# Adding x outside TensorE for 15 of 16 block groups, with six output copies on VectorE and a re-made order of steps

## The chip, the cores and the metric

The kernel runs on one core of one Trainium2 chip. The metric is the device time of one execution in microseconds (us). Every comparison below was made on one chip, with the kernel before and the other kernel in the same rounds. For one core no second core shows whether a run was disturbed, so a run counts as slow if it is over 1.5% above the fastest of its kernel, and only the other runs are compared.

## The reference

An attention without a softmax over pairs, followed by a gated layer:

```python
q_s = exp(q - max_d q);  q_s = q_s / (sum_d q_s + 1e-09)      # q, k, v: 8 x 8 x 576 x 64
k_s = exp(k - max_s k);  k_s = k_s / (sum_s k_s + 1e-09)
kv  = einsum('bhsd,bhse->bhde', k_s, v)
x   = einsum('bhsd,bhde->bhse', q_s, kv)                       # then 4608 rows x 512
H = maximum(x @ w_h, 0);  T = 1 / (1 + exp(-(x @ w_t + b_t)))
out = T * H + (1 - T) * x
```

## The kernel before

The kernel keeps x turned, with its 512 columns on partitions in four blocks, and handles the 8 batches in four pairs. Rows that don't fill a tile are done at the end as chunks 8 and 9. The gate is computed as out = x + (tanh + 1) * dd. The `blend` step writes the second term to `g`. The output tile is then turned back by matmuls with the identity, and the term x comes in at one of two places: either an elementwise addition (`add_x`) puts it into `g` first, or TensorE accumulates it with a second matmul for each block (`xs` in `turn_block`). `added(g)` lists the blocks of pair `g` that take the first way.

```python
added = lambda g: ((0, 1), (0, 1, 2), (0, 1, 2), (0, 1, 2, 3))[g]

def add_x(c, ob):
    xv, gv = views(c)
    eng = nc.vector if (c, ob) == (B - 1, 3) else nc.gpsimd
    eng.tensor_add(gv(ob), gv(ob), xv(ob))

def turn_block(t, k_, xs, us):
    dst = t[:, k_, :]
    if xs is not None:
        mm(dst, xs, ident, True, False)          # x, by TensorE
    mm(dst, us, ident, xs is None, True)

def out_tile(g, n, spare=False):
    ...
    for k_ in range(4):
        turn_block(t, k_, None if k_ in added(g) else xT[g][:, k_, n]..., gT[g][:, k_, n]...)
```

Other parts are these:

```python
def q_scale_p(b, n0, n1):                        # scaling of exp(q), on GpSimd
    e, r = eq[b][:, n0:n1], qsum[b][:, n0:n1]
    nc.gpsimd.tensor_mul(e, e, r.broadcast_to(list(e.shape)))

def q_turn(b, n0, n1):                           # batches 6 and 7: turned by DMA
    nc.sync.dma_start_transpose(out=qsD[b]..., in_=eq[b][:, n0:n1]...)

def load_bias():
    nc.sync.dma_start(brow, moe_b_t.rearrange("(k p) -> k p", p=P))   # 2 KB

def gate_bias():                                 # one small matmul on TensorE
    nc.tensor.matmul(t, brow, id4, is_transpose=True, ...)
    nc.vector.tensor_scalar_mul(bt2, t, 0.5)

def warm_up(n):                                  # fillers: results are not used
    for _ in range(n):
        mm(warm, ident, wide, True, True)
```

A list `order` of some 560 steps fixes the order of instructions by hand. Each engine works through its own steps in that order.

The softmax here doesn't subtract the row's maximum and nothing guards it: scores larger than these inputs give would overflow.

## Time and profile before

| | before |
|---|---|
| median of 3 runs | 125.06 us (124.79 to 125.07) |
| profiled run | 124.45 us, span 122.5 us, mean granted TensorE clock 0.999 |
| busy share: TensorE, VectorE, ScalarE, GpSimd | 91%, 78%, 76%, 65% |
| matmuls, VectorE, ScalarE, GpSimd instructions | 1371, 179, 130, 75 |
| sums of batch 1 (k by v) start | 28.11 us |
| first product from transposed q of batch 6 | 85.04 us |
| first 512-column product of batch 7 | 95.18 us |
| last matmul of the output starts | 118.13 us |

In the profile, PE is TensorE's matmul, PEld its weight load, DVE is VectorE, ACT ScalarE, POOL GpSimd, SP the engine that issues most transfers. `qsD` is transposed q of batches 6 and 7, `px` their product with kv, `psk` the sums over k and v, `pt` and `ph` the two halves of the gate, and `nat` an output tile. In a timeline a row is a group of like instructions, and the bracket at its end is the idle time of that engine before it and what ended it. For the last rows of the table I read TensorE's timeline.

### The profile page before, as it was taken

To read this page: it belongs to the slowest core of one execution; us is meant where nothing else is said; L and a number is where in the kernel's file an instruction comes from. 1 tells how busy PE (TensorE), PEld (TensorE's weight loads), DVE (VectorE), ACT (ScalarE), POOL (GpSimd) and SP (SyncE) were. 2 spreads that over 40 slices of the span, in tenths; PEclk is the share of its full clock that TensorE was granted. 3 is DMA by queue.
4 is the path that set the end of the run, shared out by engine and by line. 5 is a ranking of instruction groups with operands and counts; after the bars stand their busy time and mean duration, and the time that the engine had idled before them with its cause. 6 is when DMAs were issued, how large, how long until landed. Compare 5 with 4: busy or idle time off the path is not lost.

```text
span 122.5 us, 3361 instructions
## 1 busy us (share of the span) xinstructions
PE 111.3 (91%) x1371; PEld 61.5 (50%) x1371; DVE 95.9 (78%) x179; ACT 92.9 (76%) x130; POOL 79.8 (65%) x75
## 2 busy tenths in 40 slices
PE   4998985998999998999997999997999999999960
PEld 1344543354336444745745464454456545599830
DVE  1079796579999999999979996898656379779960
ACT  4193737496979998789979999983986895588650
POOL 2000487952279989599899899996995307934620
PEclk9999999999999999999999999999999999999999
DMA  3999999999999999999999999999977500539995
GB/s 100 388 402 408 409 399 397 410 412 411 406 412 409 402 411 412 415 398 416 417 356 404 411 411 401 418 212 246 438 171 214 219 0 0 206 144 390 423 384 175
DMA packets 20583, 41.24 MB, mean 337 GB/s; under 512 B 5460, under 2 KB 5976, under 8 KB 19544
## 3 DMA queue, kind: packets, MB, share of 16 engines
q1 hardware_dynamic: 20568, 41.03, 89.0%
q8 instruction: 10, 0.16, 0.5%
q14 instruction: 5, 0.04, 0.1%
HBM read 30.41 MB, written 9.44 MB: 325 GB/s over the span
## 4 chain that ended last, share of the span: by engine, by line
DMA 51%; PE 28%; ACT 5%; POOL 5%; SPq 3%; DVE 3%; issue 2%; ACTq 0%; POOLq 0%
DMA q<-in_q_dram 24%; DMA k<-in_k_dram 12%; PE ph L64 11%; DMA w32h<-in_moe_w_h_dram 9%; PE pt L64 9%; DMA qsD<-eq 6%; PE nat L64 5%; ACT eq L174 4%; SPq L94 3%; POOL eq L254 3%; POOL g L424 2%; PE px L64 1%; DVE r L224 1%; ACT xT L357 1%; PE psk L64 1%
## 5 line engine op out<-in xcount | busy, mean ns | idle before, releaser
L64 PE MATMUL pt<-xT,w16t 128*128 128x512 f16 x128 | 32.9, 380 | 0.4 <-ACT xT L361 0.3
L254 POOL TENSOR_TENSOR eq<-eq,r 128x1024 f16<-128x1024 f16 (+2 forms) x16 | 29.9, 1876 | 4.7 <-DVE r L242 1.6
L64 PE MATMUL ph<-xT,w16h 128*128 128x512 f16 x128 | 32.5, 379 | 0.4 <-DVE dd L405 0.2
L424 POOL TENSOR_TENSOR g<-g,xT 128x512 f16<-128x512 f16 x23 | 26.0, 1154 | 7.1 <-DVE g L413 4.9
L392 ACT ACTIVATE pt<-pt,bt 128x512 f32<-128x512 f32 (+1 forms) x40 | 24.8, 632 | 6.2 <-PE pt L64 5.2
L413 DVE SCALAR_TENSOR_TENSOR g<-pt,dd 128x512 f16<-128x512 f32 (+1 forms) x40 | 24.9, 632 | 4.9 <-ACT pt L392 4.3
L405 DVE SCALAR_TENSOR_TENSOR dd<-xT,ph 128x512 f16<-128x512 f16 x32 | 21.1, 677 | 6.7 <-PE ph L64 6.6
L174 ACT ACTIVATE eq<-q 128x1152 f16<-128x1152 f32 x16 | 18.3, 1168 | 7.1 <-DMA q<-in_q_dram 7.1
L185 POOL CAST v<-v 128x1152 f16<-128x1152 f32 x12 | 13.7, 1154 | 13.2 <-DMA v<-in_v_dram 12.8
L64 PEld LDWEIGHTS <-w16h 128*128 128x128 f16 x160 | 14.5, 98 | 13.2 <-issue 1.6
L64 PEld LDWEIGHTS <-w16t 128*128 128x128 f16 x160 | 14.3, 98 | 12.7 <-issue 1.1
L224 DVE TENSOR_REDUCE r<-eq 128x18 f32<-128x1152 f16 x12 | 16.0, 1345 | 6.0 <-ACT eq L174 6.0
L464 ACT COPY o<-nat 128x512 f32<-128x512 f32 x28 | 16.8, 601 | 4.4 <-PE nat L64 3.5
L174 ACT ACTIVATE ek<-k 128x1152 f16<-128x1152 f32 x16 | 18.4, 1175 | 1.6 <-DMA k<-in_k_dram 1.5
L64 PE MATMUL warm<-wide,ident 128*128 128x512 f16 x53 | 15.1, 427 | 1.8 <-DVE wide L144 1.8
L64 PE MATMUL nat<-ident,g 128*128 128x128 f16 x142 | 14.9, 219 | 0.2 <-DVE o L485 0.2
L64 PEld LDWEIGHTS <-g 128*128 128x128 f16 x144 | 11.4, 98 | 4.8 <-issue 0.5
L357 ACT CAST xT<-px 128x1024 f16<-128x1024 f32 x10 | 10.3, 1034 | 1.8 <-PE px L64 1.8
L64 PEld LDWEIGHTS <-ident 128*128 128x128 f16 x58 | 5.6, 106 | 8.4 <-issue 3.4
L69 PE MATMUL pq<-ident,eq 128*128 128x128 f16 x108 | 9.0, 219 | 0.9 <-DVE x L309 0.4
L274 DVE COPY qsT<-pq 128x1024 f16<-128x1024 f16 (+1 forms) x18 | 9.7, 542 | 0.0
L69 PEld LDWEIGHTS <-eq 128*128 128x128 f16 x108 | 7.1, 97 | 5.0 <-POOL eq L254 1.1
(53 smaller groups left out, 102.9 us busy)
## 6 DMA issues: line engine op xcount, KB each, us to landing
out_dram<-o SPq DMA_DIRECT2D x8, 1024.0 KB, 5.5
q<-in_q_dram SPq DMA_DIRECT2D x7, 1152.0 KB, 13.9
k<-in_k_dram SPq DMA_DIRECT2D x7, 1152.0 KB, 12.9
v<-in_v_dram SPq DMA_DIRECT2D x5, 1152.0 KB, 14.6
v<-in_v_dram SPq DMA_DIRECT2D x6, 576.0 KB, 11.7
q<-in_q_dram SPq DMA_DIRECT2D x2, 576.0 KB, 4.0
k<-in_k_dram SPq DMA_DIRECT2D x2, 576.0 KB, 6.7
w32h<-in_moe_w_h_dram SPq DMA_DIRECT2D x4, 256.0 KB, 9.9
```

The source lines that it names most:

```text
L64: mm = lambda o, l, r, st, sp: nc.tensor.matmul(o, l, r, start=st, stop=sp, skip_group_check=True)
L69: nc.tensor.matmul(o, i, ident, is_transpose=True, start=True, stop=True, skip_group_check=True,)
L174: nc.scalar.activation(dst[b][:, :, 2 * a : 2 * a + 2, :], in32[which][b][:, 2 * a : 2 * a + 2].rearrange("p c n d -> p n c d"), AF.Exp,)
L185: nc.gpsimd.tensor_copy(o, i)
L224: nc.vector.reduce_sum(qsum[b][:, :, h], eq[b][:, :, h, :], axis=AX.X)
L254: nc.gpsimd.tensor_mul(e, e, r.broadcast_to(list(e.shape)))
L357: copy[how](dst, t.rearrange("p c (n d) -> p c n d", d=64))
L392: nc.scalar.activation(ps, ps, AF.Tanh, bias=bt2[:, ob : ob + 1], scale=0.5)
L405: nc.vector.scalar_tensor_tensor(dd, xv(ob), -0.5, ps, op0=ALU.mult, op1=ALU.max)
L413: nc.vector.scalar_tensor_tensor(gv(ob), th, 1.0, dd, op0=ALU.add, op1=ALU.mult)
L424: eng.tensor_add(gv(ob), gv(ob), xv(ob))
L464: copy(rows_of_four((g, n // 4))[:, n % 4, :], nat.pop((g, n)))
```

## The change

The intent is to take work off TensorE, the busiest engine. x is added by an elementwise engine for all blocks but block 3 of the last pair. Four of these additions go to VectorE and the others to GpSimd. Six of the large output copies (of 32; four before) are done by VectorE, and the list of steps is made anew near the old places.

```diff
+    copy_by = {"A": nc.scalar.copy, "V": nc.vector.tensor_copy}
 ...
-    added = lambda g: ((0, 1), (0, 1, 2), (0, 1, 2), (0, 1, 2, 3))[g]
+    added = lambda g: (
+        (0, 1, 2, 3),
+        (0, 1, 2, 3),
+        (0, 1, 2, 3),
+        (0, 1, 2),
+    )[g]
-    def add_x(c, ob):
+    def add_x(c, ob, eng="P"):
         xv, gv = views(c)
-        eng = nc.vector if (c, ob) == (B - 1, 3) else nc.gpsimd
-        eng.tensor_add(gv(ob), gv(ob), xv(ob))
+        by[eng].tensor_add(gv(ob), gv(ob), xv(ob))
 ...                                    (order: all of it is re-made; the places that matter)
-        ("exp_half", 0, "q", 1), ("load_bias",), ("warm_up", 24), ("load", 1, "q"),
-        ("load", 0, "v", 2), ...
+        ("load", 1, "q"), ("load", 0, "v", 2), ("exp_half", 0, "k", 0), ...
+        ("q_trans", 0, 0), ("cast_v", 0, 0), ("load_bias",), ("q_copy", 0, 0),
+        ("gate_bias",), ("load_weight", "h", "k32", 4), ("load_weight", "t", "q32"),
 ...
+        ("kv_norm", 6), ("q_sums", 7, 0), ("carry", 5, 3), ("add_x", 4, 0, "P"), ...
+        ("q_recip", 7), ("q_scale_p", 7, 4, 9), ("out_tile", 1, 2), ("out_copy", 1, 2, "V"),
+        ("q_turn", 7, 4, 9), ("x_pair", 6, 0, True), ("diff", 5, 2), ("add_x", 4, 3, "P"),
+        ("q_scale_p", 7, 0, 4), ("exp_half", 7, "k", 0), ...
```

## The prediction

> **What bounds the kernel now.** I read, in this order: the page's busy shares and slices, the chain of waits that ended last, the groups of instructions, and the timelines of TensorE and GpSimd.
>
> ```profile
> PE 111.3 (91%) x1371; PEld 61.5 (50%) x1371; DVE 95.9 (78%) x179; ACT 92.9 (76%) x130; POOL 79.8 (65%) x75
> ...
> PE   4998985998999998999997999997999999999960
> ...
> POOL 2000487952279989599899899996995307934620
> ...
> DMA  3999999999999999999999999999977500539995
> ```
>
> TensorE is full nearly everywhere, GpSimd is full from about 35 to 90 us, and DMA is full only until about 80 us. So three limits lie close together, and the stage matters. The chain of waits gives the stages:
>
> ```profile
> 32.33 14.60 DMA k<-in_k_dram
> 46.93 15.05 DMA q<-in_q_dram
> ...
> 77.49 7.51 DMA qsD<-eq
> ...
> 85.04 0.22 PE px_l L64 x2
> ...
> 116.61 0.46 ACT pt L392
> ...
> 118.11 0.48 ACT o L485
> ```
>
> Loads rule up to 62 us; GpSimd's scaling of batch 6 and its DMA transposes stand before 85.0; from there to 116.6 the chain is TensorE alone, without a wait. The 31.6 us from 85.0 to 116.6 can shrink only by less TensorE work, or by starting earlier.
>
> Was TensorE already saturated before 85 us? Its timeline, where the last bracket is real idleness:
>
> ```profile
> 21.80 2.47 PE L64 MATMUL pt<-xT,w16t 128*128 128x512 f16 x8
> 65.25 0.41 PE L64 MATMUL px<-qsT,kvn 64*64 64x512 f16 x4 [0.89 <-ACT xT L357]
> 85.04 0.22 PE L64 MATMUL px_l<-qsD,kvn 64*64 64x64 f16 x2 [0.70 <-DMA qsD<-eq]
> 111.97 1.06 PE L64 MATMUL nat<-ident,g 128*128 128x128 f16 x16
> 112.87 1.47 PE L64 MATMUL ph<-x,w16h 128*128 128x256 f16 x12
> ```
>
> The starts matter, not the modelled ends. Sixteen output matmuls start at 111.97 and the next group at 112.87: 0.90/16 = 56 ns each. I added start-to-start gaps beyond the streaming time of every group (216 ns for a 512-column matmul, as 0.86 us per four in the chain): from the first gate at 21.8 us to the last output matmul at 118.1 us they come to roughly 6 to 7 us (about half of it gaps of 0.1 us after short groups). So TensorE has been the backlog since about 22 us; work taken off it counts, if its inputs come no later.
>
> **What the Trainium skill says.** (1) "TensorE: Matmul & The Clock Gate", Back-to-back issue gap: a warm matmul of N columns takes N/2.4 GHz plus about 2.5 ns, 56 ns at N=128; the page also gives about 81 ns in a stream with weight loads. The trace agrees with 56 ns. (2) "SBUF — State Buffer": VectorE and GpSimd share a port pair under an exclusive lock, and a VectorE instruction with two SBUF inputs contends with a GpSimd instruction that reads SBUF. The trace fits: the sum tree's second add took 0.42 us at 16.73 us but 1.13 us at 14.06 us, beside a GpSimd cast. So a VectorE add of x may cost 0.42 us or over 1 us. (3) "DMA: Bandwidth & Descriptors", HWDGE ordering: each engine's ring is consumed in order. Loads land in their order of issue here too, so an earlier issue of an output delays what is behind it.
>
> **The change part by part.**
>
> ```profile
> L424 POOL TENSOR_TENSOR g<-g,xT 128x512 f16<-128x512 f16 x23 | 26.0, 1154 | 7.1 <-DVE g L413 4.9 <-PE px L64 2.3
> L424 DVE TENSOR_TENSOR g<-g,xT 128x512 f16<-128x512 f16 x1 | 0.4, 418 | 0.0
> L464 DVE COPY o<-nat 128x512 f32<-128x512 f32 x4 | 2.6, 682 | 0.0
> L64 PE MATMUL nat<-ident,xT 128*128 128x128 f16 x32 | 6.2, 219 | 0.0
> ```
>
> *TensorE.* x is added by TensorE today for blocks 2 and 3 of the first pair and block 3 of the next two: 4 blocks x 8 tiles = the 32 matmuls of the last row. After, only block 3 of the last pair is left: 8. That removes 24 x 56 ns = **1.34 us**. (The row's 219 ns is latency, and 6.2 us would be wrong.) Of these, 16 go before about 78 us, 16 more from pairs two and three, and 8 are added in the end stage. Fillers after the first real work go from 3 pairs to 1 (4 x 216 ns = 0.9 us) and 2 at the end go; fillers partly fill waits, so I count **0.4 us**.
>
> *GpSimd.* Pair adds rise from 24 to 30, of which VectorE gets 4 instead of 1: GpSimd 23 to 26, 3 x 1.154 = +3.5 us, and one head cast more (+0.75 us). Up to the scaling of batch 6 it has 12 adds instead of 10, so about +3.0 us with the cast. Its idle stretch before 32.79 us (4.5 us) takes two adds, 2.3 us; the rest must come out of about 2.8 us of small waits between 44 and 77 us. I expect that scaling to end at 76 to 79 us (now 77.0), so the transposes land near 84.5 us (now 85.0): a gain of **0.2 us**, with a real risk of a loss.
>
> *VectorE and ScalarE.* VectorE: 3 adds x 0.418 = 1.25 us more; big output copies 4 to 6 and one fewer of the small row's, about +0.7 us; two weight casts leave (-1.2 us), x copies and remainder copies about cancel. ScalarE: two weight casts come (+1.2 us), two output copies go (-1.2 us), one 1.03 us copy of x goes. After 85 us ScalarE is busy 3.4 to 4.4 of every 5 us until 115 us and VectorE 2.6 to 4.9, so I count this as off the path there.
>
> *The new order at the start.* This is my main doubt. Now:
>
> ```profile
> 21.35 1.62 POOL L117 CAST w16t<-w32t 128x512 f16<-128x512 f32 x2 [0.86 <-DMA w32t<-in_moe_w_t_dram]
> 22.93 1.90 POOL L254 TENSOR_TENSOR eq<-eq,r 128x1024 f16<-128x1024 f16 x1
> ```
>
> Before these, at 18.20 us, GpSimd had already scaled the first part of batch 1. After, both weight casts stand ahead of both scalings. The weights still land near 21.3 us (same bytes ahead of them), so casts end at 22.97, the first scaling at 24.9, the second, with a head cast between, at 27.4 us. ScalarE has its two casts of the same weights ahead of the last copy of x, so the first gate can start only at 23.6 us, not 21.8; then TensorE meets a transpose that waits until 24.9. Walking on by hand, the sums of batch 1's k and v start at about 30.3 instead of 28.1 us with the same six gate and carry groups done. So **+2.0 us** early. It is not all lost: now there are waits later for data and for full engines (0.89 and 0.70 us above, some 1.5 us of smaller ones after 28 us), and a TensorE that is late finds its inputs ready. I let **1.7 us** be absorbed.
>
> *Loads.* The last v load stands after the batch 6 transposes now (issued at 81.65 us or later); after, all loads are ahead of all outputs, landing by about 78 us: 31.45 MB moved by 80 us in the stretches now, against 29.7 MB of loads and weights. It helps batches 5 and 7, but TensorE didn't wait for those. Counted as zero.
>
> Sum: -1.34 - 0.4 - 0.2 + 2.0 - 1.7 = -1.64 us; 125.06 - 1.6 = **123.4 us**.
>
> **The rivals.** *GpSimd becomes the bound.* For it: nearly full from 35 to 90 us, 1.15 us per add against 56 ns x 8 = 0.45 us of TensorE for what each two adds replace per block. Against: it idles from 96 to 102 us and at 28 to 33 us. If each of its extra adds delays the transposes, they land 2 to 3 us later and the result is 125 to 126 us. *The late start is not absorbed:* then all 2.0 us stand, and it is 125 us. *Everything fits better:* if TensorE reaches batch 6's product with its inputs ready at 82 us, only the shorter rest (33.1 us from 85.04 to the last output matmul at 118.1, less 0.5 us net of the removed and added matmuls there) follows, and it is 121 to 122 us. A drain of outputs at the end is unlikely to matter: DMA stands idle around 98 to 105 us, and the same four large outputs follow.
>
> **Range and chances.** The terms that I sized by hand (2.0, 1.7, 0.2) can each be off by 1 us or so, about 1.5 us together. 8 in 10: 121.6 to 125.4 us. Two per cent faster is under 122.56 us, half a spread below my value: 0.28. Slower by 2% (127.56 us) needs two rivals at once: 0.04. Within: 0.68.
>
> **What would show it.** The x matmuls of the output tiles should number 8. The first gate should start near 23.6 us, after a wait for ScalarE's copy of x, and a transpose wait for GpSimd to 24.9 us. Batch 6's second scaling should end at 76 to 79 us; the first product from transposed q should start near 84.5 us. From there to the last matmul it should be 32 to 33 us without waits. The prediction fails if GpSimd waits stand in the chain after 85 us (slower), or if the first gate starts no later than now (faster).

## The result, and the profile after

The changed kernel took 124.31 us as the median of 4 runs (124.20 to 124.61), against 125.06 us (124.79 to 125.14) for the kernel before. The ratio is 0.9947, with a 95% interval of 0.9925 to 0.9970. Every ratio in this document is the mean time of one kernel's fast runs over that of the other's of the same rounds, so it is not quite the ratio of the medians quoted beside it. The time lies in the predicted range, but the gain is 0.66 us by the ratio (0.75 us by the medians), and not the 1.64 us of the sum.

The page of the changed kernel shows the following busy times, slices and costliest group:

```profile
PE 109.6 (89%) x1335; PEld 60.3 (49%) x1335; DVE 97.1 (79%) x177; ACT 93.0 (76%) x134; POOL 83.8 (68%) x79
...
PE   4999067999899999899999999999999899999920
...
POOL 2000096887549999999999999958999128736600
PEclk9999955589999999999999999999999999999997
...
L429 POOL TENSOR_TENSOR g<-g,xT 128x512 f16<-128x512 f16 x26 | 29.9, 1166 | 8.3 <-DVE g L414 6.8
```

TensorE lost 36 matmuls, 24 for x and 12 fillers. GpSimd gained 4 us of work, with 26 additions in the place of 23 and each as long as before. What the prediction did not expect is in the PE and PEclk rows. In slices 5 to 8 (12 to 25 us) TensorE stands still, and then works at half its clock. The groups by line have these two rows:

```profile
L64 PE MATMUL nat<-ident,xT 128*128 128x128 f16 x8 | 1.8, 219 | 0.0
...
L429 DVE TENSOR_TENSOR g<-g,xT 128x512 f16<-128x512 f16 x4 | 3.1, 777 | 0.0
```

Eight matmuls for x are left, as intended. The four additions on VectorE take 777 ns on average, and not the 418 ns of the one that stood in the kernel before.

Here is the start in TensorE's timeline:

```profile
15.59 0.26 PE L135 MATMUL bias_t<-id,brow 4*128 4x4 f32 x1 [3.04 <-DMA brow<-in_moe_b_t_dram]
...
19.28 1.20 PE L64 MATMUL psk<-v,ek 64*64 64x65 f16 x72 [1.61 <-DVE qsT L274]
...
22.85 2.00 PE L64 MATMUL pt<-xT,w16t 128*128 128x512 f16 x4
...
30.75 0.44 PE L64 MATMUL psk<-v,ek 64*64 64x65 f16 x30
```

The first gate starts at 22.85 us, later than before (21.80) but sooner than predicted (23.6). The sums of batch 1 start at 30.75 us, 2.64 us later than before. However, the reason is another than the predicted weight casts. TensorE waits 3.04 us for the 2 KB of the bias. The new order issues that load behind q of batch 1 and v of batch 0. The four starts at 22.85 us take 1.8 us to the next group where they would take 0.86 us at full clock. The stretches of TensorE's granted clock give 0.51 for 15 to 20 us and 0.50 for 20 to 25 us, and 1.00 in both before.

The Trainium skill ("TensorE: Matmul & The Clock Gate", Part 1: The HAM clock gate) says that an idle window of about 3.4 us takes TensorE's clock to half, and about 3.4 us of sustained work brings it back. The trace fits this roughly. In finer stretches half clock begins at 15.1 us, 2.6 us into the wait of 3.04 us, so less idleness than 3.4 us was enough here. It ends at 25.4 us. The return took longer, about 10.2 us, with the second wait of 1.61 us in between.

The chain of waits that ended last shows where the rest went. These are pieces of it:

```profile
4.50 11.04 DMA brow<-in_moe_b_t_dram
...
82.91 0.42 DVE kvn L213
83.33 1.26 DVE r L224
84.59 0.59 DVE dd L406
85.19 0.30 DVE r L242
...
85.62 2.33 POOL eq L254
87.95 1.29 POOL g L429
89.24 1.86 POOL eq L254
...
91.13 4.30 DMA qsD<-eq
...
95.47 0.41 PE px L64 x4
```

Before, this chain held the transposes of batch 6 (they ended at 85.0 us) and TensorE alone after that. Now it holds those of batch 7. VectorE's sums of batch 7's q release GpSimd's first scaling at 85.62 us. GpSimd then does an addition of x (1.29 us), then the second scaling, then the DMA transposes take 4.30 us. TensorE's first full product of batch 7 waits for them. The addition in the middle is block 3 of batch 4, one of those that the change took off TensorE.

An addition at this place is not new in itself. The kernel before had one there too, of block 0 of batch 5, as its GpSimd timeline shows:

```profile
83.74 1.91 POOL L254 TENSOR_TENSOR eq<-eq,r 128x1024 f16<-128x1024 f16 x1 [1.22 <-DVE rz L212]
85.60 1.15 POOL L424 TENSOR_TENSOR g<-g,xT 128x512 f16<-128x512 f16 x1
86.71 2.33 POOL L254 TENSOR_TENSOR eq<-eq,r 128x1280 f16<-128x1280 f16 x1
```

What is new is that the chain starts later. VectorE's reciprocal of batch 7's sums, for which the first scaling waits, ends at 85.47 us where it ended at 83.57 us. (The bracket above names the short `rz` that VectorE did next.) The first scaling starts 1.88 us later, and the second ends at 91.10 us where it ended at 89.04 us. The last transpose lands at 95.4 us where it landed at 93.7 us. The kernel before reached batch 7's product 1.5 us after that landing. The changed kernel reached it before the landing. TensorE's timelines, first the kernel before and then the changed one:

```profile
95.18 0.40 PE L64 MATMUL px<-qsD,kvn 64*64 64x512 f16 x2
...
95.47 0.41 PE L64 MATMUL px<-qsD,kvn 64*64 64x512 f16 x4 [0.55 <-DMA qsD<-eq]
```

The table compares stages (starts in TensorE's timelines; the last column is an experiment that comes below):

| us | before | after | a_add43 |
|---|---|---|---|
| sums of batch 1 | 28.11 | 30.75 | 29.90 |
| first product of batch 6 | 85.04 | 84.71 | 84.22 |
| first 512-column product of batch 7 | 95.18 | 95.47 | 94.21 |
| idle before it, for the transposes | none | 0.55 | none |
| last matmul of the output | 118.13 | 117.91 | 116.68 |
| span | 122.5 | 122.8 | 121.5 |

From batch 6's product to batch 7's the kernel before took 10.14 us and the changed one 10.76 us. The change lost its gain in this stage. From batch 7's product to the last matmul it went from 22.95 to 22.44 us. TensorE now waits 0.70 us for the last blend just before the last three matmuls, but the kernel before lost about as much there in smaller gaps: its last 2.16 us hold 0.87 us of gate matmuls and 11 output matmuls of 56 ns, which leaves 0.67 us. (The profiled run of the changed kernel is its slowest of four, 124.61 us, and that of the kernel before its fastest, which is why the spans are in the other order than the medians.)

VectorE pays for its additions. These are the first two in its timeline:

```profile
72.91 0.83 DVE L429 TENSOR_TENSOR g<-g,xT 128x512 f16<-128x512 f16 x1
...
74.86 1.35 DVE L429 TENSOR_TENSOR g<-g,xT 128x512 f16<-128x512 f16 x1
```

The other two take 0.51 and 0.42 us. Together that is 3.1 us for four, or 1.4 us more than four times 0.42. This is the contention at the shared port pair that the prediction took from the Trainium skill ("SBUF — State Buffer", Who interferes with whom), and this trace agrees with it. All four start while GpSimd adds or scales. The first three each end 0.28 us after that GpSimd instruction does (at 73.46, 75.93 and 87.95 us), so their length is what was left of it and a little more. The fourth started 0.12 us before such an end and took 0.42 us, as one does beside an idle GpSimd. GpSimd loses time as well: the addition between batch 7's scalings, which runs into the third, takes 1.33 us and not its usual 1.15 us.

How full the middle stage is can be read from the busy times in stretches. Each entry is busy us with the number of instructions in parentheses, then the granted clock, the share of DMA time and the rate. First the kernel before:

```profile
45.00:80.00 35.00, 33.80 (x484) 18.84 (x478) 32.05 (x57) 32.84 (x43) 32.35 (x23) 1.00 1.06 404
```

Then the changed kernel:

```profile
45.00:80.00 35.00, 34.59 (x512) 18.28 (x513) 34.50 (x60) 34.40 (x45) 34.71 (x25) 1.00 1.05 410
```

The entries are PE, PEld, DVE, ACT, POOL. Before, VectorE and GpSimd had about 3 us free in these 35 us. After, no engine has as much as 0.7 us free. The change fills the stage to the brim on four engines at once.

### The profile page after: what moved, and what is told of

Read it like the earlier page. It is cut to its first block, busy times and chain, and to the rows that moved or that the text cites. A ratio compares the mean times of both kernels' runs of the same rounds, so it can differ in the third digit from the quotient of the medians.

```text
span 122.8 us, 3295 instructions
## 1 busy us (share of the span) xinstructions
PE 109.6 (89%) x1335; PEld 60.3 (49%) x1335; DVE 97.1 (79%) x177; ACT 93.0 (76%) x134; POOL 83.8 (68%) x79
## 4 chain that ended last, share of the span: by engine, by line
PE 61%; DVE 13%; DMA 12%; POOL 4%; SPq 3%; issue 1%; ACT 1%; DVEq 1%; POOLq 0%
PE pt L64 21%; PE ph L64 20%; DMA brow<-in_moe_b_t_dram 9%; PE nat L64 6%; PE px L64 4%; PE pq L69 4%; DMA qsD<-eq 4%; POOL eq L254 3%; PE psk L64 3%; DVE r L224 3%; SPq L94 3%; DVE g L414 3%; DVE dd L406 2%; DVE qsT L274 1%; PE px_l L64 1%
## 5 line engine op out<-in xcount | busy, mean ns | idle before, releaser
L429 POOL TENSOR_TENSOR g<-g,xT 128x512 f16<-128x512 f16 x26 | 29.9, 1166 | 8.3 <-DVE g L414 6.8
L254 POOL TENSOR_TENSOR eq<-eq,r 128x1024 f16<-128x1024 f16 (+2 forms) x16 | 30.1, 1887 | 3.7 <-PE px_l L64 3.0
L468 ACT COPY o<-nat 128x512 f32<-128x512 f32 x26 | 15.1, 597 | 7.4 <-PE nat L64 7.4
L64 PE MATMUL warm<-wide,ident 128*128 128x512 f16 x41 | 12.1, 446 | 1.8 <-DVE wide L144 1.8
L64 PE MATMUL nat<-ident,g 128*128 128x128 f16 x142 | 13.4, 219 | 0.0
L64 PEld LDWEIGHTS <-g 128*128 128x128 f16 x144 | 10.5, 98 | 5.6 <-DVE g L414 0.9
L69 PE MATMUL pq<-ident,eq 128*128 128x128 f16 x108 | 9.9, 234 | 0.3 <-DVE kvn L213 0.3
L358 ACT CAST xT<-px 128x1024 f16<-128x1024 f32 x9 | 9.3, 1028 | 1.2 <-PE px L64 1.1
L69 PEld LDWEIGHTS <-eq 128*128 128x128 f16 x108 | 7.7, 106 | 4.5 <-issue 1.4
L64 PE MATMUL psk<-v,ek 64*64 64x65 f16 x576 | 7.1, 200 | 1.7 <-DVE qsT L274 1.6
```

The lines of the kernel that those rows point to most:

```text
L64: mm = lambda o, l, r, st, sp: nc.tensor.matmul(o, l, r, start=st, stop=sp, skip_group_check=True)
L69: nc.tensor.matmul(o, i, ident, is_transpose=True, start=True, stop=True, skip_group_check=True,)
L429: by[eng].tensor_add(gv(ob), gv(ob), xv(ob))
L468: copy_by[eng](rows_of_four((g, n // 4))[:, n % 4, :], nat.pop((g, n)))
```

## The experiments

I had three theories for the missing microsecond. The **start**: the wait for the bias and the half clock cost it. **Batch 7**: the work on VectorE and GpSimd ahead of batch 7's transposes costs it, above all the addition between the two scalings. **Full engines**: the elementwise engines are full before 80 us, so TensorE's relief is worth little. Runs named a_, c_ and s_ are variants of the changed kernel, b_ of the kernel before. All gave correct results. A median below is over all executions of a run, the slow ones included. The kernel before took 125.05, 125.29, 125.56 and 125.42 us (medians) in the four sets of rounds, and each ratio is against it.

### Set 1: the start

**a_bias** issues the bias load ahead of q of batch 1, as before the change.

```diff
+("load_bias",),
 ("load", 1, "q"), ("load", 0, "v", 2), ...
-("q_trans", 0, 0), ("cast_v", 0, 0), ("load_bias",), ("q_copy", 0, 0),
+("q_trans", 0, 0), ("cast_v", 0, 0), ("q_copy", 0, 0),
```

> The changed kernel with one step moved: the 2 KB bias load is issued before batch 1's q load, as in the kernel before, instead of behind q and v. Theory (the bias holds up TensorE's in-order queue for 3.0 us at 12.5 us, its clock falls to half from 15.5 to 25.7 us, and this is what took the gain): no wait for the bias, full clock throughout, first gate near 23 us but its four matmuls 0.9 instead of 1.8 us, the first sums of batch 1's k and v at about 29.7 instead of 30.75 us; time 123.2 to 123.7 us, ratio to the kernel before 0.985 to 0.990. Rival (the casts of the second weight ahead of batch 1's scaling hold the start, as I predicted): first gate and the sums move by less than 0.3 us, time 124.1 to 124.4 us.

It took 124.86 us (124.25 to 125.66), ratio 0.9992 [0.9948, 1.0036], which is no gain and a miss. TensorE's timeline tells why:

```profile
16.84 0.48 PE L64 MATMUL psk<-v,ek 64*64 64x65 f16 x36 [3.32 <-DVE qsT L274]
```

The wait for the bias is gone, but another of 3.32 us, for VectorE's copy of transposed q, takes its place. The clock still falls to half. The sums of batch 1 start at 30.1 us. At batch 7's product TensorE waits 0.94 us for the transposes, so that it starts at 95.48 us, when it started at 95.47 us in the changed kernel.

**a_gate** leaves the load where it is and moves the bias step of TensorE behind the first product.

```diff
-("gate_bias",), ("load_weight", "h", "k32", 4),
+("load_weight", "h", "k32", 4),
 ...
-("cast_weight", "h", 3, "A", 0.5), ("q_trans", 0, 2, "nat"),
+("cast_weight", "h", 3, "A", 0.5), ("gate_bias",), ("q_trans", 0, 2, "nat"),
```

> The changed kernel with the bias load left late, but the step that transposes the bias on TensorE moved behind the first product, where the bias has long landed. Theory: the same result as with the earlier load, 123.2 to 123.8 us, since what costs is the wait in TensorE's and VectorE's order, not the place in the DMA queue. If instead the DMA order itself mattered (what else moved in the queue), this would stay at 124.2 us while the earlier load gains.

It took 124.92 us (123.83 to 125.87, the highest slow), ratio 0.9963 [0.9918, 1.0008], again a miss. The wait before the first sums is 2.30 us, the clock is at half for a shorter time, and the sums of batch 1 start at 29.5 us, 1.3 us sooner than in the changed kernel. Nothing of that shows in the times. (In its profile, which is of its fastest run, the last matmul comes 0.6 us sooner than in the changed kernel's, which is of its slowest.)

**a_fill** keeps TensorE busy with fillers in both waits, so that its clock holds.

```diff
-("gate_bias",), ...
+("warm_up", 14), ("gate_bias",), ...
-("kv_half", 0, 1),
+("warm_up", 9), ("kv_half", 0, 1),
```

> The changed kernel with 14 filler matmuls ahead of the bias transpose and 9 ahead of batch 0's sums: the waits for the bias (3.0 us) and for the copy (1.6 us) stay, but TensorE is busy in them. If the loss is through the clock falling to half: full clock throughout, 123.3 to 123.9 us. If it is through the waits alone: 124.2 us or later, as in the changed kernel.

It took 123.66 us (123.40 to 125.00), ratio 0.9905 [0.9861, 0.9949]. The clock is now full, and the sums of batch 1 start at 30.0 us. The ratio is 0.4% below that of the changed kernel, but the intervals overlap. TensorE's timeline shows a new wait where the prediction had looked for one, at batch 6:

```profile
85.31 0.41 PE L64 MATMUL px<-qsD,kvn 64*64 64x512 f16 x4 [0.46 <-DMA qsD<-eq]
```

**b_bias** does the reverse. It gives the kernel before the late bias load, and nothing else.

```diff
-("exp_half", 0, "q", 1), ("load_bias",), ("warm_up", 24), ("load", 1, "q"),
-("load", 0, "v", 2), ("cast_v", 0, 0),
+("exp_half", 0, "q", 1), ("warm_up", 24), ("load", 1, "q"),
+("load", 0, "v", 2), ("load_bias",), ("cast_v", 0, 0),
```

> The kernel before with one step moved the other way: the bias load issued behind batch 0's v. Theory: TensorE waits about 3 us for the bias near 12 us, its clock falls to half for about 10 us, and the time rises by 0.5 to 1.5 us to 125.6 to 126.6 us. Rival (the weight casts): no change, 125.0 us.

It took 127.65 us (127.11 to 128.02), ratio 1.0211 [1.0172, 1.0250], so the same late load costs 2.6 us there, more than I had expected.

```profile
15.88 0.26 PE L135 MATMUL bias_t<-id,brow 4*128 4x4 f32 x1 [4.08 <-DMA brow<-in_moe_b_t_dram]
```

The sums of batch 1 start at 31.5 us and batch 7's product at 98.2 us, so that the 3 us pass through the whole kernel. In the kernel before a late start is not absorbed, while in the changed one three different cures of it bring nothing that is clearly measurable. So the late start is a real event, but it isn't the missing time, at least not while something else binds later.

### Set 2: batch 7, and the additions alone

**after2** is the changed kernel once more, for the comparison within this set.

```diff
(no edit)
```

> The changed kernel again, unchanged but for the layout of its list of steps, as the yardstick on this chip: ratio to the kernel before 0.992 to 0.998, half clock from about 15.5 to 25.7 us, the first product of batch 7 at about 95.5 us after a wait for the transposes.

It took 124.49 us (124.08 to 125.27), ratio 0.9946 [0.9902, 0.9991]. The result repeats. TensorE's wait for batch 7's transposes is 0.92 us in its profile.

**a_q7** tries to give batch 7's transposes all the room. Its sums, reciprocals and both scalings are moved ahead of what stood between them.

```diff
 ("q_sums", 7, 1),
+("q_sums", 7, 0), ("q_recip", 7), ("cast_v", 7, 1),
+("q_scale_p", 7, 4, 9), ("q_scale_p", 7, 0, 4), ("kv_norm", 6),
 ("out_tile", 1, 0), ...
 ("q_turn", 7, 4, 9),
+("q_turn", 7, 0, 4),
 ("x_pair", 6, 0, True), ...
-(the same steps at their later places)
```

> The changed kernel with batch 7's two sums, its reciprocal and both GpSimd scalings moved together, ahead of two blends on VectorE and with no add of x between the scalings (batch 6's normalisation keeps its time). Theory (the chain VectorE sums, GpSimd scaling, transposes of batch 7 has become the bound at 95.5 us, and it hides any gain made earlier): transposes land near 91 us, no wait before batch 7's product, which starts at 94.3 to 94.8 us; 123.4 to 124.0 us, 0.3 to 0.9 us under the changed kernel of this job. Rival (only the slow start counts): the same time as the changed kernel within 0.2 us.

It took 125.78 us (125.10 to 126.11), ratio 1.0034 [0.9991, 1.0077]. It is slower than the changed kernel, which is a miss. The wait for batch 7's transposes is gone indeed, but VectorE now does the second sums (1.26 us) and the reciprocals ahead of the steps that free TensorE's accumulators, and TensorE waits for those:

```profile
83.85 1.02 PE L64 MATMUL ph<-xT,w16h 128*128 128x512 f16 x4 [1.88 <-DVE dd L406]
```

Batch 6's product moves to 87.0 us and batch 7's to 96.8 us. The edit had moved a wait from one place of a full engine to another.

**a_best** puts together all that I then held for improvements: a_gate with ten fillers, the moves of a_q7, batch 6's second scaling directly behind the first, and the last blend ahead of a copy.

```diff
 (a_gate and a_q7, and:)
+("warm_up", 10), ("kv_half", 0, 1),
 ("q_scale_p", 6, 0, 4),
+("q_scale_p", 6, 4, 9),
 ...
+("blend", 9, 3),
 ("tile9_copy", 3, 3, "V"),
-("blend", 9, 3),
```

> The changed kernel with four moves: the bias transpose behind the first product and 10 filler matmuls in the wait that is left (full clock at the start), the batch 7 moves of the run above, the second scaling of batch 6 directly behind the first, and the last blend ahead of the copy before it. Theory (start and transposes both bind, so that each alone gains little and both together more): first sums of batch 1's k and v at 28.7 to 29.5 us, no wait for transposes, batch 7's product at 93 to 94 us, last output matmul at about 116 us; 122.4 to 123.2 us, 1.2 to 2.0 us under the changed kernel. Rival (each gain is independent and the transposes count for nothing): at most 0.7 us under it, as the fillers alone gave.

It took 125.71 us (124.85 to 127.27, two of six slow), ratio 1.0012 [0.9959, 1.0064]. This is a miss too, by the same cause: batch 6's product comes at 87.0 us.

**a_noadd** takes the new additions back and keeps the new order. TensorE adds x where it did before, and has its 24 matmuls back.

```diff
-    (0, 1, 2, 3), (0, 1, 2, 3), (0, 1, 2, 3), (0, 1, 2),
+    (0, 1), (0, 1, 2), (0, 1, 2), (0, 1, 2, 3),
-("add_x", 0, 2, "P"), ("add_x", 0, 3, "P"), ("add_x", 1, 2, "P"), ("add_x", 1, 3, "P"),
-("add_x", 2, 3, "V"), ("add_x", 3, 3, "P"), ("add_x", 4, 3, "P"), ("add_x", 5, 3, "V"),
+("add_x", 6, 3, "P"), ("add_x", 7, 3, "V"),
```

> The changed kernel with the additions of x as in the kernel before (12 of 16 blocks off TensorE, one of the last adds on VectorE), in the new order: 24 output matmuls more on TensorE, 8 adds fewer on GpSimd and VectorE up to pair three, 2 more in the last pair. If TensorE alone bounds: 1.34 us slower than the changed kernel of this job. Theory (the transposes of batch 7 bind at 95.5 us, and without the adds they come 1.3 us or more sooner): 0.2 to 0.8 us slower. If the adds cost as much as they save: the same.

It took 124.74 us (124.44 to 125.24), ratio 0.9968 [0.9923, 1.0012]. Against after2 that is 0.25 us more by the medians. The ratios give the same, with an uncertainty of about 0.8 us. Taken at face value, the additions, which are the point of the change, are worth 0.25 us, while the matmuls that they replace stand for 24 x 56 ns = 1.34 us. Batch 7's product starts at 95.76 us without a wait. In the changed kernel it starts 0.3 us earlier, and with a wait. GpSimd's first scaling of batch 7 starts at 85.37 us here, almost as late as in the changed kernel, so it is the new order, and not the additions taken off TensorE, that starts this chain late. Both batch 7 and full engines could explain that so little is left.

### Set 3: which engine, and the one addition

**s_pe**, **s_dve** and **s_pool** each add useless work to one engine of the changed kernel, in the gates (or diffs) of batches 2 and 3, well before 80 us. They add eight matmuls of 216 ns (1.73 us), eight fills on VectorE of 272 ns (2.2 us), or eight fills on GpSimd of 317 ns (2.5 us).

```diff
 (s_pe, in gate)
+        if c in (2, 3):
+            mm(ps, w16["t"][:, 0, ob * P : ob * P + P], xv(0), True, False)
 (s_dve, in diff; s_pool: nc.gpsimd, a tile half as wide)
+        if c in (2, 3):
+            nc.vector.memset(idle, 0.0)
```

> The changed kernel with TensorE loaded alone: the first of the four matmuls of each gate of batches 2 and 3 is issued twice (8 x 216 ns = 1.73 us, between 45 and 80 us, same result). If TensorE is the bound in that stage, as I predicted: 1.3 to 1.7 us over the changed kernel, ratio to the kernel before about 1.006 to 1.009. If VectorE is the bound there: under 0.6 us over it, ratio 0.994 to 0.999.

> The changed kernel with VectorE loaded alone: one memset of an unused 128x512 tile behind each of the 8 differences of batches 2 and 3 (8 x 0.2 to 0.27 us, 1.6 to 2.2 us in sum). If VectorE is the bound from 45 to 80 us: 1.3 to 2.2 us over the changed kernel, ratio 1.005 to 1.012. If TensorE is: under 0.6 us over it.

> The changed kernel with GpSimd loaded alone: one memset of an unused 128x256 tile behind each of the same 8 differences, 1.6 to 3 us in sum. If the chain of GpSimd's scaling and the transposes is the bound (it runs full from 45 to 80 us): the transposes of batch 6 come later by about as much, and the time is 1 us or more over the changed kernel. If VectorE or TensorE is: under 0.6 us over it.

s_pe took 125.62 us, ratio 1.0005 [0.9970, 1.0040]; s_dve took 125.35 us, ratio 0.9997 [0.9955, 1.0040]; s_pool took 125.82 us with two of seven runs slow (134.7 and 135.1), ratio of the fast ones 1.0007 [0.9967, 1.0046]. Against the changed kernel's 0.9947 that is 0.5 to 0.6% for each, or about 0.7 us, whichever engine gets the load. None of the three expectations had this. The three don't differ beyond their intervals, so nothing here points to a single engine that paces the stage. The profiled runs of s_pe and s_dve show more. Batch 6's sums start at 81.7 and 81.8 us, where they started at 79.6 us (79.7 us in after2), so a delay as large as the added work is there at this point. (For s_dve it needn't all be the added work: its profiled run is its slowest, 126.56 us, and a microsecond late from the start.) Batch 7's product then starts at 96.8 us without a wait in s_pe, only 1.3 us later than the changed kernel's. Some 0.6 us were swallowed by the wait that had stood there. In s_dve it still stands, at 0.65 us.

**a_add43** changes one thing. The addition of block 3 of batch 4 goes behind GpSimd's second scaling of batch 7.

```diff
-("add_x", 4, 3, "P"),
 ("q_scale_p", 7, 0, 4),
+("add_x", 4, 3, "P"),
```

> The changed kernel with one step moved: the GpSimd add of batch 4's block 3 (1.33 us) goes behind batch 7's second scaling instead of between the two scalings; VectorE's order is untouched. Theory (the transposes of batch 7 are what TensorE waits for at 95.5 us): they land 1.3 us sooner, the wait before batch 7's product is gone, it starts 0.6 to 0.8 us sooner and the time falls by 0.5 to 0.8 us, ratio 0.988 to 0.991. If something else paces that stage: the same as the changed kernel.

It took 123.88 us (123.37 to 124.01), ratio 0.9863 [0.9831, 0.9895]. This interval lies wholly below those of the changed kernel, 0.9947 [0.9925, 0.9970] and 0.9946 [0.9902, 0.9991]. The exchange of two neighbouring steps is worth 0.84% of 125 us, about 1.0 us, give or take 0.5 by the two intervals. GpSimd's timeline now has both scalings in one row, without the addition between:

```profile
85.13 4.37 POOL L254 TENSOR_TENSOR eq<-eq,r 128x1280 f16<-128x1280 f16 x2 [0.42 <-DVE r L242]
```

TensorE's timeline has the product of batch 7 without a bracket, 1.26 us earlier than the 95.47 us of the changed kernel:

```profile
94.21 0.40 PE L64 MATMUL px<-qsD,kvn 64*64 64x512 f16 x2
```

Not all of these 1.26 us can be the edit's, since 0.49 us are there already at batch 6's product (84.22 for 84.71 us), ahead of the exchanged steps; that much is a difference between two runs. From batch 6's product to batch 7's it is 9.99 us for 10.76 us, so the trace gives the exchange 0.77 us, within what the times give.

This confirms the batch 7 theory by its own lever: with the addition out of the chain, the wait is gone. It doesn't test what made the chain start late, which the traces put down to VectorE's later sums. No run moved those alone; a_q7 moved them together with the scalings.

The run also says what the additions are worth: against a_noadd (0.9968) the difference is 1.05%, or 1.3 us with an uncertainty of about 0.7 us, and 24 matmuls of 56 ns are 1.34 us. The two ratios come from different sets, but their intervals don't overlap. So full engines did not take most of the gain, though the uncertainty leaves room for a part. The stage before 80 us is full, but it did not eat the relief as a whole.

### Set 4: the start again, with batch 7 out of the way; and the additions in the old order

If the late start was hidden only by the wait at batch 7, then cures of it should show now. **c_fill** is a_add43 with the fillers of a_fill. **c_gate** is a_add43 with a_gate and ten fillers. **c_all** is c_gate with batch 6's second scaling directly behind its first, and the last blend ahead of a copy.

```diff
 (c_fill = a_add43 +)
+("warm_up", 14), ("gate_bias",), ... ("warm_up", 9), ("kv_half", 0, 1),
 (c_gate = a_add43 +)
-("gate_bias",), ("load_weight", "h", "k32", 4),
+("load_weight", "h", "k32", 4), ... ("warm_up", 10), ("kv_half", 0, 1), ...
+("gate_bias",), ("q_trans", 0, 2, "nat"),
 (c_all = c_gate +)
 ("q_scale_p", 6, 0, 4),
+("q_scale_p", 6, 4, 9), ... ("blend", 9, 3), ("tile9_copy", 3, 3, "V"),
```

> The changed kernel with the GpSimd add of batch 4's block 3 behind batch 7's second scaling, and with the 14 and 9 filler matmuls in the two waits of the start (full clock, the waits themselves stay). If the half clock at the start still costs once batch 7's transposes no longer bind: 0.3 to 1.0 us under the run with the moved add alone, ratio to the kernel before 0.979 to 0.984. If it is absorbed by 80 us: the same as that run, 0.984 to 0.988.

> The moved add, the bias transpose behind the first product, and 10 fillers in the wait that is left: neither the bias wait nor the half clock. First sums of batch 1 at about 29 us. If the late start counts: ratio 0.976 to 0.983. If the stage from 30 to 80 us is paced by the three engines together and the transposes of batch 6 (84 to 85 us) come next: 0.984 to 0.988, and a wait for the transposes stands before batch 6's product.

> The run above with batch 6's second scaling directly behind its first (two adds go behind it) and the last blend ahead of the copy before it. If the transposes of batch 6 bind in the run above, they come 2 us sooner here and it is 0.5 to 1.5 us faster than that run. If not, the same within 0.4 us, or slower where the two adds that went back hold up output tiles.

c_fill took 123.85 us, ratio 0.9882 [0.9835, 0.9928], with full clock throughout. c_gate took 123.72 us, ratio 0.9865 [0.9820, 0.9910]; it was to be free of the half clock, but still ran at 0.50 from 20 to 25 us, as did c_all. c_all took 123.56 us (123.22 to 123.66), ratio 0.9846 [0.9810, 0.9883]. None of them is distinguishable from a_add43. In these three, in a_add43 and in the three of set 1 the sums of batch 1 start between 29.5 and 30.9 us, and those of batch 6 between 78.9 and 79.7 us. The later starts mostly have the later sums of batch 6, so that about half of a difference of 1.4 us at the start is left before 80 us. It is not a fixed relation: after2 starts at 29.4 us and has its sums of batch 6 at 79.7 us. In the times no such difference shows. How full that stage is after an earlier start shows the stretch of c_gate:

```profile
50.00:80.00 30.00, 29.59 (x457) 16.05 (x459) 29.36 (x51) 29.23 (x39) 29.62 (x22) 1.00 1.07 408
```

c_all has the lowest ratio and beats both kernels, by 1.5% the kernel before. Shown to matter in it is the exchange of a_add43; the rest isn't shown to bring anything.

**b_adds** is the last question: was the new order needed? It makes the new additions in the kernel before, each behind its blend, two of them on VectorE, and leaves all else.

```diff
-    added = lambda g: ((0, 1), (0, 1, 2), (0, 1, 2), (0, 1, 2, 3))[g]
+    added = lambda g: ((0, 1, 2, 3), (0, 1, 2, 3), (0, 1, 2, 3), (0, 1, 2))[g]
-        eng = nc.vector if (c, ob) == (B - 1, 3) else nc.gpsimd
+        eng = nc.vector if (c, ob) in ((2, 3), (5, 3)) else nc.gpsimd
 (and in order, for the new blocks)
 ("blend", 0, 2),
+("add_x", 0, 2),
 ...
```

> The kernel before with the additions of x alone as in the change (15 of 16 blocks), each new add directly behind its blend, no other step moved, two of them on VectorE. TensorE loses 24 output matmuls. If the adds alone gave the gain: 123.7 us, ratio 0.989. If the new adds delay GpSimd's scalings and the output tiles that wait for them, as I expect without a new order: 1.000 to 1.015.

It took 130.03 us (129.72 to 130.98), ratio 1.0375 [1.0330, 1.0419]. I had the direction, but not the size. TensorE now waits for GpSimd's additions inside output tiles, here for one at 78 to 81 us:

```profile
79.52 0.23 PE L64 MATMUL nat<-ident,g 128*128 128x128 f16 x1 [1.28 <-POOL g L424]
80.62 0.34 PE L64 MATMUL nat<-ident,g 128*128 128x128 f16 x3 [0.87 <-POOL g L424]
```

Batch 6's product comes at 89.0 us and batch 7's at 99.7 us. An addition of 1.15 us on a full engine needs a long lead ahead of the tile that reads it. The new order has such a lead; which of its many moves gives it was not tried.

## Why the prediction was right or wrong

**TensorE, −1.34 us: right in mechanism, and in size as far as it is shown.** Eight matmuls for x are left, the price of 56 ns each stands, and a_add43 against a_noadd shows 1.3 us for the 24, give or take 0.7, once batch 7's wait is gone. The prediction was also right that TensorE's relief counts. It failed in not seeing where that would be stopped.

**"TensorE alone, without a wait" from batch 6's product on: the step that failed.** The prediction followed GpSimd to batch 6's second scaling (expected to end at 76 to 79 us, measured 75.9) and to that batch's product (expected near 84.5 us, measured 84.71). From there to the last matmul it reckoned with TensorE alone, "32 to 33 us without waits". Measured are 33.20 us with a wait of 0.55 us (0.92 us in after2) for batch 7's transposes. The prediction did not follow batch 7's chain at all; its remark on batch 7, that "TensorE didn't wait for those", is about loads. This chain starts 1.88 us later than before, at VectorE's reciprocal, then has an addition of 1.3 us between its two scalings and transposes of 4.3 us. With that addition moved by one step, the time falls by 1.0 us (0.77 us in the trace). The ratio of 0.9863 is then a gain of 1.7 us. That this comes so near to 1.64 us is in part luck, since other terms were off as well. The rival "GpSimd becomes the bound" named a mechanism of this kind ("each of its extra adds delays the transposes"), but with the transposes that stood in the chain, those of batch 6, in mind and with another size. The sign of failure that it gave, GpSimd waits in the chain after 85 us, is in the chain at 85.62 to 91.1 us.

**The text held two sums.** Its list of terms gives 1.64 us. Its own stages give less: batch 6's product at 84.5 us is a gain of 0.5 us (of which the list books 0.2), and "0.5 us net" less from there on makes 1.0 us. Even that 0.5 is too much: by the timelines 20 of the matmuls for x stood before batch 6's product and 12 after it, where 8 are added, so 4 x 56 ns = 0.22 us are saved there. (The two fillers at the end stood behind the last output matmul.) The list counts the 20 and the fillers in full, although the product can start no sooner than its transposes land. I should have seen that the two differ. The stages would have given 0.7 us, near the measured 0.66, but not for the right reason. In the profiles batch 6's product came 0.33 us earlier, and from there to the last matmul the changed kernel took 33.20 us where the kernel before took 33.09 us: up to batch 7's product it lost 0.62 us, most of it in the wait for the transposes, and after it won 0.51 us. In a_add43 the gains up to batch 6's product and from there on are 0.82 and 0.63 us.

**The late start, +2.0 us: size nearly right by luck, cause wrong.** Measured were 2.64 us at the sums of batch 1. The weight casts do stand ahead of GpSimd's scaling, but they take 1.17 us for two and not 1.62, and the first scaling starts at 22.04 us. What held TensorE was the bias: the prediction looked at the order of large loads and not at that of the smallest one, which waited 11.04 us behind the loads issued before it. After the wait TensorE ran at half its clock up to 25.4 us. I had read the granted clock of the kernel before, which is full, and not asked what a wait of 3 us would do to it.

**Absorbed, −1.7 us: about that.** At batch 6's product the changed kernel is 0.33 us ahead in spite of its late start, so it made up 2.97 us. The 20 matmuls of 56 ns that are gone before it explain 1.12 us, if they count in full, which leaves about 1.85 us as an estimate of what was absorbed. Cures of the start, with or without the wait at batch 7, bring nothing clear (a_bias, a_gate, c_fill, c_gate). The reason given, later waits that a late TensorE finds already over, fits. Why the kernel before does not absorb the same late load (b_bias, 2.6 us) isn't settled: the two orders differ in too much. Also open is a_fill's 0.4%, which c_fill doesn't confirm.

**VectorE and ScalarE, off the path: wrong for VectorE.** The additions cost 3.1 us for four and not 0.42 each. The prediction had named the possibility and then used the short time. VectorE's sums of batch 7 are the first pieces of the chain that binds, and they are what starts it 1.9 us later than before.

**Range and chances.** The result of 124.31 us is within 121.6 to 125.4, and "within 2%", given 0.68, is what came. The rivals had covered the upper side with the right kind of event at the wrong batch.

## What to carry to other kernels

When work is taken off the busiest engine and given to one that is nearly full, follow the receiving engine to every later product that depends on it, not only to the one that binds today: a step of 1.3 us between two halves of a chain, where such a step had caused no wait before, cost here about 1.0 us once the new order started that chain 1.9 us later, and an exchange of two neighbouring steps brought it back. In a re-made order check the smallest loads too, since a 2 KB load waited here for 11.04 us behind what was issued ahead of it, and TensorE, which waited for it, lost its clock as well as its time.

## What the Trainium skill lacked or had wrong

- "TensorE: Matmul & The Clock Gate" gives about 3.4 us of idleness for the fall to half clock. Here half clock began 2.6 us into an idle time of 3.04 us (0.51 of full speed from 15 to 20 us). It gives about 3.4 us of sustained work for the return; here, with work that a further wait of 1.61 us broke up, half clock lasted about 10.2 us, to 25.4 us, and in a_add43, with waits of 2.19 and 2.47 us, 6.8 us. The page has no figure for such mixed stretches, which is what a kernel with short waits needs.
- "SBUF — State Buffer" describes the lock between VectorE and GpSimd, but gives no price for the addition of two 128x512 fp16 tiles under it. The four in this trace took 0.83, 1.35, 0.51 and 0.42 us; the first three ended 0.28 us after the GpSimd instruction that ran when they started.
- "DMA: Bandwidth & Descriptors", HWDGE ordering, says that descriptors are consumed in ring order. It doesn't give the consequence in time for a tiny load: 2 KB took 11.04 us from issue to landing behind the loads issued before it (4.6 MB, of which part had landed by then).
- No page that I read treats how much lead a slow engine's step needs ahead of its reader. Here the additions put right behind their blends in the old order cost 3.75%, while the changed kernel, whose order differs in much else too, gained 0.5%.
